# A gated mix of a state-space convolution and a dense layer: later signal stages, more store buffers, accumulators seeded by ScalarE, and a new list schedule

## The chip, the cores and the metric

The kernel runs on one core of a Trainium2 chip. The metric is device time in microseconds (us), the median of several runs. The core has a matrix engine (PE, with weight loads shown as PEld), a vector engine (DVE), a scalar engine (ACT), GpSimd (POOL) and SyncE (SP). SP does no arithmetic here; it issues most of the transfers, and POOL issues the rest. Each engine works through its own instructions in the order in which the program lists them.

## The reference

Input x is 2048 x 512 (sequence by channels). Three things are made of it and mixed:

```python
g = sigmoid((x * gate_w).sum(-1, keepdims=True))
# a: a long convolution over the sequence, one kernel K per channel (N = 128 states)
dt = exp(log_dt); P = exp((dt * A)[:, :, None] * l)       # complex, l = 0 .. 2047
K = einsum("dn,dnl,dn->dl", C, P, dt * B).real
a = irfft(rfft(pad(x)) * rfft(pad(K)))[:2048] + x * Dskip
# b: a dense layer of 512 -> 1792 -> 512
b = gelu(x @ w1 + b1) @ w2 + b2
out = g * a + (1 - g) * b
```

All numbers are 32-bit floats. b1 and b2 are the dense layer's two biases.

## The kernel before, in words

The program has two parts. The **front** (function `front`) runs the whole dense layer, builds the convolution's taps K, and puts both the signal and the taps through the first stage of a two-stage Fourier transform. The second part (`conv`) does the second stage, multiplies the spectra, transforms back, and adds the result to the output. `conv` is not touched by the change.

The dense layer keeps float32 accuracy by splitting every operand into a high part and a low rest (`split`: ACT or DVE casts the high part, DVE subtracts it for the rest). Each product then takes three matmuls: high x high, low x high, high x low. The sequence is cut into 8 blocks of 256 rows, and the 14 column tiles of the hidden layer into two halves of 7, so there are 16 passes (`NB`); in passes 0 to 7 the first half of w1 and w2 is resident, in 8 to 15 the second. A pass has four steps (`j` = 0 to 3) of 2, 2, 2 and 1 column tiles:

- `hidden` (matmuls in lines 899 to 901, 256 columns): 12 per column tile, into one of three PSUM banks `ph`. Then ACT applies gelu with bias b1 (line 916) and casts the high part `hh` (line 919), and DVE subtracts for `hl` (line 929).
- `output` (lines 947 to 949, 512 columns): three per column tile and row half, accumulated in two PSUM banks `acc`, one for each half of the block's 256 rows. After step 3, ACT scales the sum by (1 - g) into `io` (line 968) and it is stored. In passes 0 to 7 the accumulation starts with a matmul of a row of ones with b2 (line 942), the bias split in two parts as well (`bias`).

The taps take 16 chunks (`taps`): DVE and ACT build powers and rotations in `xc` and `y` (ACT's sines at lines 604 to 606, DVE's products up to line 667), and PE contracts them over the states (`contract`, line 681, 128 small matmuls into the bank `pk`). After every second chunk a **first stage** follows (`first_stage`, line 403): eight matmuls into four banks, one `ph`, the `pk` and two `pu`, each then copied out by ACT. The signal has eight first stages of its own (`signal`): two loads of rows of x into `ux` (line 417), the same eight matmuls, four copies by ACT into store buffers `st` (line 421), and stores to a scratch tensor `tu_d` (line 424). The buffers come from a ring of `N_ST`. Before `conv` begins, `early` reads 27 pieces of `tu_d` back into tiles called `attic`, `loft` and `den` (line 446). While the front runs, parts of these tiles serve for other things; so `attic` in a row of a profile is a store buffer, a load buffer or a `ux`, by the line that it stands with.

What sets the order is a list schedule made when the program is built. Every piece of work is a `Task` with an engine, an estimated duration, a due time and its dependencies. `Plan.run` walks the engines in time: of the tasks that are ready it takes the one with the earliest due time, adds its estimated duration, and the order found in this way is the order in which instructions are issued. Due times are linear in the step's number, bent by `warp`, with offsets: `U_0` and `U_GAP` set the signal's stages, `K_0` and `T_KG` the chunks of the taps, `T_0` and `T_MLP` the dense steps, `D_...` single kinds of task. These times are the plan's own and not the chip's.

Of the kernel before, what the change touches and what calls it, by code (L numbers as in the profile page):

```python
# [17 lines left out]
P = 128  # L18
L = 2048
D = 512  # L20
# [13 lines left out]
T_0 = 22.7  # L34
T_MLP = 411.78
K_0 = 24.88
T_KG = 373.15
U_0 = -15.83
U_GAP = 12.75
LAG = 12.23  # L40
TABLE = 9.03
D_KA = -63.09
D_KP = 0.01
D_S1 = 19.39
D_EV = -65.14
D_H = -60.13
D_LO = -10.68
PS = (2, 3, 1, 2)
N_ACC, N_H, N_PK, N_PU = PS
D_SP = 2.63  # L50
MEM = (6, 2, 3)
N_LD, N_HL, N_ST = MEM
D_XS = -33.08
D_G = 1.83
N_WARM = 13
T_EARLY, T_LOFT, T_DEN = 376.87, 422.84, 432.0
Y_K, Y_U = 41.11, 36.03
W_MLP = (-0.0634, -0.0326, 0.0273)
W_KG = (-0.0624, -0.0351, -0.0316)
W_U = (-0.058, -0.1265, 0.0001)  # L60
D_MAG = 0.58
D_ROT = 1.16
D_CON = 0.62
D_PHA = 0.72
D_PRE = 0.04
D_XL = -26.72
D_COE = 0.25
D_OUT = -5.37
N_LATE = 2
N_REST = 3  # L70
N_KEEP = 4

# [131 lines left out]
class Plan:  # L204
# [5 lines left out]
    def add(self, part, hold, fn, due, reads=(), writes=(), table=None, done=None, after=(), rows=1.0):  # L210
# [9 lines left out]
        t.rows = rows  # L220
# [10 lines left out]
    def run(self):  # L231
        clock = Clock()
        free = dict.fromkeys(("PE", "ACT", "DVE", "POOL", "SP", "GP"), 0.0)
# [4 lines left out]
        table, order, dma = None, [], 0.0  # L238
        for _ in self.tasks:
# [13 lines left out]
            hold = clock.run(at, t.hold, t.rows) if p == "PE" else t.hold  # L253
# [21 lines left out]
def gated_mix(  # L275
# [41 lines left out]
    def front(pool, psum, keep, attic, loft, den):  # L317
# [10 lines left out]
        def act(n, fn, due, reads=(), writes=(), table=None, ops=1):  # L328

            return pl.add("ACT", 0.1 * ops + n / 1200.0, fn, due, reads, writes, table)  # L330

        def mm(hold, fn, due, reads=(), writes=(), rows=1.0):

            return pl.add("PE", hold, fn, due, reads, writes, rows=rows)

        def move(kb, fn, due, reads=(), writes=(), queue="SP", after=()):

            hold = 0.45 if queue == "SP" else 1.0
            return pl.add(queue, hold, fn, due, reads, writes, done=kb / 360.0, after=after)
# [20 lines left out]
        st, ld = rooms[1 : 1 + N_ST], rooms[1 + N_ST : 1 + N_ST + N_LD]  # L360
        gwb = rooms[1 + N_ST + N_LD]
# [16 lines left out]
        b2r = pool.tile([P, D], F32R, name="b2r")  # L378
        ones = pool.tile([P, P], F32R, name="ones")
# [12 lines left out]
        def first_stage(xs, due, evac, ahead=2):  # L392
# [12 lines left out]
            mm(1.2, products, due + D_S1, [*(key for _, key in xs), "c1"], [key for _, key in banks], 0.5)  # L405
# [5 lines left out]
        def signal():  # L411
            for s in range(8):
# [6 lines left out]
                def evac(r, pp, key, s=s, t=t):  # L419
                    k = take("st", N_ST)  # L420
                    act(512, lambda: nc.scalar.copy(st[k], pp), t + D_EV, [key], [("st", k)])  # L421
# [9 lines left out]
        def early():  # L431

            us = places(attic, loft, den)
            keys = [("ux", 0)] + [("st", k) for k in range(N_ST)]
# [17 lines left out]
        def make_dt():  # L452
# [25 lines left out]
            act(4, lambda: nc.scalar.activation(r, r, AF.Exp, scale=0.25), -200, [], ["dt"], table="exp")  # L478
# [26 lines left out]
        def prepare(u, t, eb_k):  # L505
# [25 lines left out]
            act(7 * UW, scaled, act_due, ["pr"], ["xt"], ops=7)  # L531
# [6 lines left out]
            act(11 * UW, exps, act_due, ["pr"], [("ea", u % 2), kx], "exp", ops=11)  # L538
# [17 lines left out]
            act(18 * UW, sines, act_due, [], ["xt", "xv"], "sin", ops=3)  # L556
# [45 lines left out]
        def waves(t):  # L602
# [4 lines left out]

            act(99 * CW, sines, t + D_KA, ["ph"], ["tt"], "sin", ops=3)

        def begin(c, k, t):  # L610

            cs = slice(c * CW, (c + 1) * CW)
            act(
                8 * CW, lambda: nc.scalar.copy(xc[k][:, :, 0:4], x4[:, :, :, cs]), t + D_KA,  # L614
                ["x4"], [("xc", k)],
            )
# [54 lines left out]
        def contract(u, c, k, t):  # L671
# [18 lines left out]
            for g0 in (0, 4):  # L690
                mm(1.89, lambda g0=g0: products(g0), t + D_KP, ["y0", "y1", ("xc", k)], [("pk", q)])
# [8 lines left out]
            act(512, lambda: nc.scalar.copy(xs, pks[q].rearrange("p s g -> p (s g)")), t + D_S1, [("pk", q)], [key])  # L700
# [4 lines left out]
            def evac(r, pp, key):  # L705
                act(
                    512,
# [68 lines left out]
        def split(h, lo, src, hk, lk, key, due, on_vector=False):  # L776
            if on_vector:
                vec(512, lambda: nc.vector.tensor_copy(h, src), due, [key], [hk], fast=2)
            else:
                act(512, lambda: nc.scalar.copy(h, src), due, [key], [hk])  # L780
# [51 lines left out]
        def gates(b0, b1_, t):  # L832
# [3 lines left out]
                16, lambda: nc.scalar.activation(gate[:, 0, ts], gs[:, ts], AF.Sigmoid), t,  # L836
# [11 lines left out]
        def bias():  # L848

            k, q = take("ld", N_LD), take("ld", N_LD)  # L850
            one, b2f, keys = ld[k][:, 0:P], ld[q], [("ld", k), ("ld", q)]

            def fill():
                nc.gpsimd.memset(b2f, 0.0)
                nc.gpsimd.memset(one, 0.0)
                nc.gpsimd.memset(one[0:1], 1.0)
                nc.gpsimd.memset(one[32:33], 1.0)

            def rows():
                nc.sync.dma_start(b2f[0:1], b2)  # L860
                nc.sync.dma_start(b2f[32:33], b2)

            def go():
                nc.scalar.copy(ones, one)
                nc.scalar.copy(b2r, b2f)

            def low():
                nc.vector.tensor_sub(b2r[32:33], b2f[32:33], b2r[32:33].bitcast(F32))

# [468 lines left out]
```

## Time and profile before

| | |
|---|---|
| runs (us) | 539.93, 541.77, 539.12; median 539.93 |
| span of the profiled execution | 539.9 us, within 0.03 us of the median, so the two are used as one |
| instructions | 12181 |
| moved | 104.73 MB, mean 194 GB/s |
| first hidden matmul | 6.35 us |
| last hidden matmul, start | 424.25 us |
| first matmul of `conv` | 424.46 us |
| last matmul of the program, start | 528.15 us |

How the rows are read: a row of the page's groups has line, engine, operation, output <- inputs, shapes, count, then busy time, the mean of one in ns, and the idle time just before them with what ended it. A row of the timeline has its start, its duration and the instruction; `x4` means that four such are merged. Matmuls are pipelined, so a matmul's duration (0.28 or 0.39 us) is longer than its share of PE's time; the distance from one start to the next is that share. A row of waits has the waiting engine and line, what it waited for, the total, how often, and the longest. The granted clock is 1.00 when PE runs at full speed.

### The profile page before, as it was taken

The page shows a single profiled execution, that of the slowest core. Times are in us where ns is not written, and L with a number is a line of the kernel's source. Part 1 is how long each engine was busy: PE and PEld are TensorE (multiplying, and loading weights), DVE is VectorE, ACT ScalarE, POOL GpSimd, SP SyncE. Part 2 cuts the span into 40 slices and gives each one's busy share as a digit, 9 for nine tenths or more (in the row PEclk, how much of TensorE's full clock was granted, in tenths as well). Part 3 has the DMA queues.
Part 4 walks back from the last instruction along what each step waited for, and adds up shares of the span by engine and source line. Part 5 has one row for each costly group of instructions (what it writes and reads, how often), then busy time and mean ns, then how long its engine had stood idle before and what let it go on. Part 6 is the DMA issues. An engine that isn't in the chain of part 4 may idle for free.

```text
span 539.9 us, 12181 instructions
## 1 busy us (share of the span) xinstructions
PE 511.7 (95%) x4818; PEld 385.6 (71%) x4818; DVE 426.8 (79%) x806; ACT 353.5 (65%) x614; POOL 40.9 (8%) x79
## 2 busy tenths in 40 slices
PE   7878899999999999989999999999999999999981
PEld 7546789898899889777988989889888522223620
DVE  5898799999999959869999899999511388887132
ACT  4989846699875599976577987387253555555030
POOL 2000000000000000000102010101010001011040
PEclk9879999999999999999999999999999999999996
DMA  7989564162584442583887037514778758998888
GB/s 245 357 288 313 181 235 139 59 197 82 130 232 179 158 127 72 178 280 74 212 196 205 19 88 162 126 60 104 231 188 198 210 207 289 392 386 290 319 163 189
DMA packets 80837, 104.73 MB, mean 194 GB/s; under 512 B 39222, under 2 KB 43450, under 8 KB 80268
## 3 DMA queue, kind: packets, MB, share of 16 engines
q1 hardware_dynamic: 73756, 79.80, 46.7%
q0 software_dynamic: 6688, 21.79, 16.5%
q10 hardware_dynamic: 336, 2.36, 1.2%
q8 instruction: 38, 0.62, 0.4%
q14 instruction: 19, 0.16, 0.1%
HBM read 58.31 MB, written 45.62 MB: 192 GB/s over the span
## 4 chain that ended last, share of the span: by engine, by line
PE 76%; DMA 9%; ACT 8%; DVE 3%; issue 1%; SPq 1%; ACTq 0%; DVEq 0%
PE pk L681 10%; PE ph L899 8%; PE acc L947 8%; PE ph L901 8%; PE ph L900 8%; PE acc L949 7%; PE acc L948 7%; PE p2u L1108 5%; PE p2k L1108 5%; PE pa L1147 3%; PE pb L1236 3%; DMA tu_d<-attic 3%; DMA attic<-in_xs_dram 2%; PE ph L403 2%; ACT L916 1%
## 5 line engine op out<-in xcount | busy, mean ns | idle before, releaser
L899 PE MATMUL ph<-xh,wh 128*128 128x256 f32 x448 | 128.9, 288 | 3.4 <-ACT attic L421 2.2
L901 PE MATMUL ph<-xh,wl 128*128 128x256 f32 x448 | 127.6, 285 | 0.8 <-DVE wl L782 0.7
L900 PE MATMUL ph<-xlo,wh 128*128 128x256 f32 x448 | 127.2, 284 | 0.0
L899 PEld LDWEIGHTS ph<-xh,wh 128*128 128x128 f32 x448 | 85.8, 192 | 14.1 <-issue 5.6
L947 PE MATMUL acc<-wh,hh 128*128 128x512 f32 x210 | 85.1, 405 | 3.2 <-ACT hh L919 3.2
L900 PEld LDWEIGHTS ph<-xlo,wh 128*128 128x128 f32 x448 | 85.9, 192 | 2.0
L901 PEld LDWEIGHTS ph<-xh,wl 128*128 128x128 f32 x448 | 85.8, 191 | 1.6 <-DVE wl L782 1.6
L949 PE MATMUL acc<-wh,hl 128*128 128x512 f32 x210 | 83.2, 396 | 0.4 <-DVE hl L929 0.4
L948 PE MATMUL acc<-wl,hh 128*128 128x512 f32 x210 | 83.1, 396 | 0.0
L916 ACT ACTIVATE ph<-ph,b1t 128x256 f32<-128x256 f32 x112 | 50.4, 450 | 42.8 <-PE ph L901 40.8
L929 DVE TENSOR_TENSOR hl<-ph,hh 128x512 fp32r<-128x512 f32 (+1 forms) x62 | 38.5, 621 | 32.4 <-ACT hh L919 32.3
L681 PE MATMUL pk<-y,den 128*32 128x64 f32 x2048 | 61.4, 290 | 0.0
L681 PEld LDWEIGHTS pk<-y,den 128*32 128x32 f32 x2048 | 57.2, 136 | 3.7 <-issue 1.4
L947 PEld LDWEIGHTS acc<-wh,hh 128*128 128x128 f32 x210 | 39.7, 189 | 18.2 <-issue 6.8
L949 PEld LDWEIGHTS acc<-wh,hl 128*128 128x128 f32 x210 | 39.8, 190 | 11.0 <-DVE hl L929 2.1
L643 DVE TENSOR_TENSOR y<-y,ea 128x64 f32<-128x64 f32 (+4 forms) x80 | 45.5, 569 | 0.2
L948 PEld LDWEIGHTS acc<-wl,hh 128*128 128x128 f32 x210 | 39.8, 189 | 6.7
L919 ACT CAST hh<-ph 128x512 fp32r<-128x512 f32 (+1 forms) x62 | 33.0, 533 | 10.3 <-PE acc L948 6.9
L488 DVE TENSOR_TENSOR loft<-den,zz 128x256 f32<-128x256 f32 (+2 forms) x48 | 37.4, 779 | 2.7 <-ACT den L614 2.3
L489 DVE TENSOR_TENSOR loft<-den,zz 128x256 f32<-128x256 f32 (+2 forms) x48 | 37.3, 777 | 0.0
L656 DVE TENSOR_TENSOR y<-y,loft 128x2048 f32<-128x2048 f32 x16 | 36.6, 2288 | 0.0
L1116 ACT COPY k<-p2k 128x512 f32<-128x512 f32 x32 | 18.8, 586 | 25.0 <-issue 13.1
(178 smaller groups left out, 876.3 us busy)
## 6 DMA issues: line engine op xcount, KB each, us to landing
tu_d<-attic SPq DMA_DIRECT2D x64, 128.0 KB, 3.4
tk_d<-sk SPq DMA_DIRECT2D x32, 256.0 KB, 4.9
tk<-tk_d SPq DMA_DIRECT2D x32, 256.0 KB, 4.4
t_d<-sa SPq DMA_DIRECT2D x32, 256.0 KB, 4.8
t<-t_d POOLq DMA_DIRECT2D x9, 512.0 KB, 7.1
attic<-in_xt_dram SPq DMA_DIRECT2D x16, 256.0 KB, 3.8
xh_d<-xh SPq DMA_DIRECT2D x8, 512.0 KB, 3.4
xl_d<-xlo SPq DMA_DIRECT2D x8, 512.0 KB, 4.6
```

The costliest lines, as they stand in the source:

```text
L488: vec(2 * m, lambda: vv.tensor_mul(t, a, br), due, [ka, *kb], [kt])
L643: nc.vector.tensor_mul(both(n, 64 - 3 * n, n), both(0, 64 - n, n), an)
L681: nc.tensor.matmul(pks[q][32 * j : 32 * j + 32, :, gg], x[:, r, :, ch], y[:, r, :, ch], start=(r == 0), stop=(r == 1), skip_group_check=True,)
L899: nc.tensor.matmul(p, h, xh[xk][:, d], start=(d == 0), stop=False)
L900: nc.tensor.matmul(p, h, xlo[xk][:, d], start=False, stop=False)
L901: nc.tensor.matmul(p, lo, xh[xk][:, d], start=False, stop=(d == 3))
L916: nc.scalar.activation(phs[q][:, n], phs[q][:, n], AF.Gelu_apprx_tanh, bias=b1t[:, f : f + 1])
L929: nc.vector.tensor_sub(lo, phs[q][:, 0:nf], hi.bitcast(F32))
L947: nc.tensor.matmul(a, h, wh[1][w], start=start, stop=False)
L948: nc.tensor.matmul(a, h, wl[1][w], start=False, stop=False)
L949: nc.tensor.matmul(a, l, wh[1][w], start=False, stop=(j == 3))
L1108: nc.tensor.matmul(out[64 * i : 64 * i + 64], w, x, start=True, stop=True)
```

## The change

It has five parts.

- **The second bias.** The function `bias` and the matmul of ones with b2 are gone. b2 is loaded once, broadcast to all 128 partitions (`b2a`), and ACT copies it into an accumulator before the accumulation starts (`seed`): twice at the start, and right after the scaling of each block's sum in passes 0 to 6. The first output matmul then adds to what is there. The warm-up matmuls at the start now write the two accumulators rather than `pk`, twelve instead of thirteen.
- **The signal's first stage begins later**: `U_0` from -15.83 to 18.93.
- **Five store buffers** for three (`N_ST`), the two added ones are tiles of their own (`st`). The two halves of an evicted bank are stored by one transfer of 256 KB instead of two of 128 KB.
- **The gates** are computed in four batches instead of three, and the blocks at whose steps their dot products stand are listed (`DOTS_AT`).
- **The list schedule** of the front is made anew: almost all constants, the tasks' estimated durations, and a plan that knows two more things, a cost when PE changes between tiled and whole matmuls (`SWITCH`) and a limit of eight transfers under way per queue (`N_LANES`).

```diff
-U_0 = -15.83
-U_GAP = 12.75
+U_0 = 18.93
+U_GAP = 10.84
...
-MEM = (6, 2, 3)
+MEM = (6, 2, 5)
 N_LD, N_HL, N_ST = MEM
...
+DOTS_AT = (2, 6, 7, 8, 12, 18, 21, 23)
-N_WARM = 13
+N_WARM = 12
...
+N_LANES = 8
+SWITCH = 0.1
...
             if p in ("SP", "GP"):
                 dma = max(dma, at + 1.2) + t.done
-                end = dma + 0.9
+                end = dma + 1.2
+                landed[p].append(end)
+                if len(landed[p]) >= N_LANES:
+                    free[p] = max(free[p], landed[p][-N_LANES])
...
-        st, ld = rooms[1 : 1 + N_ST], rooms[1 + N_ST : 1 + N_ST + N_LD]
+        st, ld = rooms[1:4] + tiles(N_ST - 3, [P, D], "st"), rooms[4 : 4 + N_LD]
...
-                    for m in range(2):
-                        move(
-                            128, lambda m=m: nc.sync.dma_start(rows[:, 8 * s + 4 * m + r], st[k][64 * m : 64 * m + 64]),
-                            t, [("st", k)], [("u_d", 8 * s + 4 * m + r)],
-                        )
+                    at = rows[:, 8 * s + r : 8 * s + r + 5 : 4].rearrange("k m d -> m k d")
+                    move(
+                        256, lambda: nc.sync.dma_start(at, st[k]), t,
+                        [("st", k)], [("u_d", 8 * s + 4 * m + r) for m in range(2)],
+                    )
...
-        def bias():
...
+        def seed(q, due):
+
+            act(0.52, lambda: nc.scalar.copy(acc[q], b2a), due, ["b2a"], [("acc", q)])
...
-                start = j == 0
-                if start and b < NSB:
-                    nc.tensor.matmul(a, ones, b2r, start=True, stop=False)
-                    start = False
+                seeded = b < NSB
+                start = j == 0 and not seeded
...
                         t + D_EV, [("acc", q), ("gate", b % NSB)], [("io", r)],
                     )
+                    if b + 1 < NSB:
+                        seed(q, t + D_EV)
...
+            move(256, lambda: nc.sync.dma_start(b2a, b2.to_broadcast([P, D])), D_B2, [], ["b2a"])
...
-            pl.add("PE", 0.213 * N_WARM, warm, -200, ["dm"], [("pk", 0)])
+            pl.add("PE", 0.213 * N_WARM, warm, -200, ["dm"], [("acc", q) for q in range(N_ACC)])
+            for q in range(N_ACC):
+                seed(q, D_B2)
...
-            when = {1 + round(D_G * b): b for b in range(NSB)}
-            batches = {0: (0, 1), 2: (1, 3), 7: (3, 8)}
+            when = dict(zip(DOTS_AT, range(NSB)))
+            batches = {0: (0, 1), 2: (1, 3), 4: (3, 5), 7: (5, 8)}
```

The change's constants show little of what the new order is, so three places of it stand here. In these rows a number behind a name is a buffer's, and differs between the two programs for the same tile.

First place, ACT at the start of the program: the casts of x and of the weights (`xh`, `wh`), and the first gelu. Before:

```order
L780 CAST xh_106<-attic 128x512 x2
L780 CAST wh_110<-sk 128x512
L864 CAST ones<-attic 128x128
L865 CAST b2r<-attic 128x512
L780 CAST wh_117<-sk 128x512
L780 CAST wh_112<-sk 128x512
L780 CAST wh_118<-sk 128x512
L780 CAST wh_119<-sk 128x512
L780 CAST wh_114<-y 128x512
L916 ACT_TABLE_LOAD
L916 ACTIVATE ph_87<-ph_87,b1t 128x256 x2
L919 CAST hh_138<-ph_87 128x512
```

Now:

```order
L792 CAST xh_108<-attic 128x512 x2
L792 CAST wh_112<-sk 128x512
L862 COPY acc_85<-b2a 128x512
L862 COPY acc_86<-b2a 128x512
L792 CAST wh_119<-sk 128x512
L792 CAST wh_114<-sk 128x512
L905 ACT_TABLE_LOAD
L905 ACTIVATE ph_87<-ph_87,b1t 128x256 x2
L908 CAST hh_140<-ph_87 128x512
L792 CAST wh_120<-sk 128x512
L792 CAST wh_121<-sk 128x512
```

The two seeds stand where the bias was cast, and the first gelu has moved ahead of three weight casts.

Second place, ACT after the first block's gelus: the tables of the first taps (`loft<-pr`, `ea`, `den`). Before:

```order
L529 ACTIVATE loft<-pr 128x128 x7
L536 ACT_TABLE_LOAD
L536 ACTIVATE ea_98<-pr 128x128 x6
L536 ACTIVATE den<-pr 128x128 x5
L421 COPY attic<-ph_89 128x512
L421 COPY attic<-pk_90 128x512
L421 COPY attic<-pu_91 128x512
L552 ACTIVATE loft<-loft 128x768
L553 ACT_TABLE_LOAD
L553 ACTIVATE loft<-loft,half_pi 128x768
L554 ACTIVATE loft<-loft 128x768
L421 COPY attic<-pu_92 128x512
```

Now, up to the second block's first gelu:

```order
L548 ACT_TABLE_LOAD
L548 ACTIVATE ea_98<-pr 128x128 x6
L548 ACTIVATE den<-pr 128x128 x5
L848 ACT_TABLE_LOAD
L848 ACTIVATE gate<-gs 128x2
L564 ACTIVATE loft<-loft 128x768
L565 ACT_TABLE_LOAD
L565 ACTIVATE loft<-loft,half_pi 128x768
L566 ACTIVATE loft<-loft 128x768
L905 ACT_TABLE_LOAD
L905 ACTIVATE ph_88<-ph_88,b1t 128x256 x2
L908 CAST hh_140<-ph_88 128x512
```

The evictions of the signal's first stage (line 421, now 433) are gone from this place, and the first gate stands in it. Ahead of these rows stand, since the first block's last weight cast, the seven scalings, four casts of x for the second and third block, and the first block's last gelu.

Third place, SP, which issues the transfers, after the first weights. Before:

```order
L1002 DMA attic<-in_gw_dram 128x512
L1011 DMA dm<-in_dskip_dram 4x128
L417 DMA attic<-in_xl_dram 128x512
L417 DMA ux_103<-in_xl_dram 128x512
L773 DMA attic<-in_xt_dram 128x512 x2
L773 DMA attic<-in_xs_dram 128x512 x4
L417 DMA attic<-in_xl_dram 128x512
L417 DMA ux_103<-in_xl_dram 128x512
L773 DMA attic<-in_xs_dram 128x512
L424 DMA tu_d<-attic 64x512 x6
```

Now:

```order
L988 DMA attic<-in_gw_dram 128x512
L1000 DMA dm<-in_dskip_dram 4x128
L785 DMA attic<-in_xt_dram 128x512 x4
L429 DMA attic<-in_xl_dram 128x512
L429 DMA ux_105<-in_xl_dram 128x512
L785 DMA attic<-in_xs_dram 128x512 x2
L828 DMA xh_d<-xh_109 128x1024
L785 DMA attic<-in_xs_dram 128x512
L828 DMA xl_d<-xlo_111 128x1024
```

The x of the second and third block (`in_xt`) is now loaded ahead of the signal's rows (`in_xl`), and the stores of the signal's first stage (line 424, now 436) have left this stretch of the queue.

More of the change, by code (lines that the diff above doesn't have):

```diff
@@ L232, in run @@
         clock = Clock()
-        free = dict.fromkeys(("PE", "ACT", "DVE", "POOL", "SP", "GP"), 0.0)
+        free = dict.fromkeys(("PE", "ACT", "DVE", "POOL", "SP", "GP"), 0.75)
         ready = {p: [] for p in free}
@@ L237, in run @@
                 ready[t.part].append(t)
-        table, order, dma = None, [], 0.0
+        table, tiled, order, dma = None, False, [], 0.0
+        landed = {"SP": [], "GP": []}
         for _ in self.tasks:
@@ L252, in run @@
             ready[p].remove(t)
-            hold = clock.run(at, t.hold, t.rows) if p == "PE" else t.hold
+            hold = t.hold
+            if p == "PE":
+                turn = SWITCH if t.tiled != tiled else 0.0
+                tiled = t.tiled
+                hold = clock.run(at, turn + hold, t.rows)
             if t.table and t.table != table:
@@ L377, in front @@
         dm = pool.tile([P, P], F32, name="dm")
-        b2r = pool.tile([P, D], F32R, name="b2r")
-        ones = pool.tile([P, P], F32R, name="ones")
+        b2a = pool.tile([P, D], F32, name="b2a")
         dts = tiles(4, [P, 4], "dts")
@@ L477, in make_dt @@
             vec(300, before, -200, [], ["dt"])
-            act(4, lambda: nc.scalar.activation(r, r, AF.Exp, scale=0.25), -200, [], ["dt"], table="exp")
+            act(0.1, lambda: nc.scalar.activation(r, r, AF.Exp, scale=0.25), -200, [], ["dt"], table="exp")
             vec(400, behind, -200, [], ["dt"])
@@ L706, in evac @@
                 act(
[L707 removed]
+                    0.48,
                     lambda: nc.scalar.copy(
@@ L846, in gates @@
             )
-        def bias():
[L850 to L868, printed above, removed]
-            pl.add("POOL", 0.5, fill, -99, [], keys)
-            pl.add("SP", 0.9, rows, -98.5, [], keys, done=0.1)
-            act(640, go, 0, keys, ["b2"], ops=2)
-            vec(512, low, 0, keys, ["b2"])
+        def seed(q, due):
+            act(0.52, lambda: nc.scalar.copy(acc[q], b2a), due, ["b2a"], [("acc", q)])
         def cols(i):
```

125 lines of the change are left out of this document (62 added, 63 removed).

## The prediction

> **What bounds the kernel now.** I read the page's busy shares first, then the stretches, then PE's waits early and late. The page, under 1:
>
> ```profile
> PE 511.7 (95%) x4818; PEld 385.6 (71%) x4818; DVE 426.8 (79%) x806; ACT 353.5 (65%) x614; POOL 40.9 (8%) x79
> ```
>
> PE leads, but a mean hides where time is lost. The stretches (start:end, length, then busy time and count of each engine, granted clock, DMA share, GB/s):
>
> ```profile
> 6.35:15.40 9.05, 7.17 (x48) 6.13 (x49) 6.63 (x12) 4.28 (x8) 0.57 (x1) 1.00 0.94 307
> 15.40:17.80 2.40, 0.44 (x4) 0.12 (x2) 2.00 (x5) 2.32 (x5) 0.00 (x0) 1.00 1.04 399
> 17.80:22.70 4.90, 4.90 (x13) 3.60 (x14) 4.49 (x9) 4.84 (x14) 0.68 (x2) 0.65 1.04 375
> ...
> 28.40:36.40 8.00, 4.11 (x16) 0.69 (x16) 7.87 (x22) 7.69 (x10) 0.00 (x0) 0.77 0.94 289
> 36.40:41.00 4.60, 4.53 (x30) 4.39 (x36) 4.14 (x7) 2.33 (x4) 0.00 (x0) 0.65 0.95 342
> ...
> 80.00:120.00 40.00, 40.00 (x475) 35.53 (x474) 40.00 (x77) 29.85 (x51) 0.25 (x2) 1.00 0.43 140
> ...
> 200.00:240.00 40.00, 40.00 (x408) 34.76 (x401) 32.57 (x70) 36.42 (x71) 1.31 (x4) 1.00 0.54 175
> ```
>
> From 80 us on PE is filled at full clock (two of the rows shown). Before that it idles, the clock is granted at 0.65 to 0.77 in three stretches, and DMA is near its limit. So the front, up to its last matmul, is PE-bound behind a bad first 66 us. How bad needs PE's own pace:
>
> ```profile
> 60.84 0.39 PE L948 MATMUL acc<-wl,hh 128*128 128x512 f32 x1
> 61.07 0.39 PE L949 MATMUL acc<-wh,hl 128*128 128x512 f32 x1
> ...
> 95.03 0.64 PE L403 MATMUL ph<-s,c1t 32*64 32x512 f32 x2
> ...
> 96.07 0.50 PE L947 MATMUL acc<-wh,hh 128*128 128x512 f32 x1
> ...
> 253.37 0.28 PE L900 MATMUL ph<-xlo,wh 128*128 128x256 f32 x1
> ...
> 253.49 0.28 PE L901 MATMUL ph<-xh,wl 128*128 128x256 f32 x1
> ```
>
> Start to start, a 512-column matmul takes 0.23 to 0.235 us, a 256-column one 0.12 (0.1175 over longer runs), a whole first stage 1.04. What PE did up to 66 us (groups in that window, with their counts and idle time):
>
> ```profile
> L899 PE MATMUL ph<-xh,wh 128*128 128x256 f32 x56 | 17.1, 306 | 3.4 <-ACT attic L421 2.2 <-DVE wh L778 1.1
> ...
> L947 PE MATMUL acc<-wh,hh 128*128 128x512 f32 x20 | 8.5, 427 | 2.0 <-ACT hh L919 2.0
> L949 PE MATMUL acc<-wh,hl 128*128 128x512 f32 x19 | 8.2, 430 | 0.0
> ...
> L403 PE MATMUL pu<-attic,c1t 32*64 32x512 f32 x12 | 6.2, 691 | 2.4 <-ACT attic L421 2.4
> ...
> L403 PE MATMUL ph<-attic,c1t 32*64 32x512 f32 x6 | 3.2, 608 | 1.4 <-DMA attic<-in_xl_dram 1.4
> L942 PE MATMUL acc<-b2r,ones 128*128 128x512 f32 x4 | 1.9, 480 | 1.8 <-ACT io L968 1.8
> ```
>
> 168 hidden matmuls (3 x 56) x 0.1175 = 19.7; 58 output ones (20 + 19 + 19) x 0.235 = 13.6; 4 bias ones 0.9; three first stages 3.1. That is 37.4 us of work in the 59.7 us from the first hidden matmul at 6.35: **22.3 us lost**. The rows name 10.9 us of waits; the low clock cost 4.9 x 0.35 + 8.0 x 0.23 + 4.6 x 0.35 = 5.2. After 66 us PE waits by the list for just this:
>
> ```profile
> PE acc L947 <- ACT hh L919: 1.2, 1, 1.2
> PE acc L949 <- DVE hl L929: 0.4, 1, 0.4
> ```
>
> The contractions, on the page:
>
> ```profile
> L681 PE MATMUL pk<-y,den 128*32 128x64 f32 x2048 | 61.4, 290 | 0.0
> ```
>
> That is 3.84 us for each of the 16 (128 matmuls). The same sum for 66 to 424.4 us, by the loops' counts, gives 1176 x 0.1175 + 572 x 0.235 + 61.4 + 13 x 1.04 + 12 x 0.235 = 350.3 of 358.4: 8.1 us of small overheads. The second part (424.5 on) is the same code before and after.
>
> **The change part by part.** *The bias matmuls go.* 16 at 0.235 us: **-3.8**, all on PE while it is full. In their place ACT makes 16 copies 128x512. A PSUM to SBUF copy of that size is in this row, with a table load:
>
> ```profile
> 39.15 0.59 ACT L421 COPY attic<-pu 128x512 f32<-128x512 f32 x1 [2.25 <-DMA tu_d<-attic]
> 39.76 1.28 ACT L916 ACT_TABLE_LOAD   x1
> 41.05 0.45 ACT L916 ACTIVATE ph<-ph,b1t 128x256 f32<-128x256 f32 x1
> ...
> 41.80 1.14 ACT L780 CAST xh<-attic 128x512 fp32r<-128x512 f32 x2
> ```
>
> No copy of 512 elements into PSUM stands in this trace. Its bounds are the 0.45 of the half-sized gelu, which does write PSUM, and the 0.64 of a scaled read out of it (1.28 for two, below); I take the 0.59 of the copy the other way, 9.4 us in all. The new order has 54 table loads on ACT for 47: 7 x 1.28 = 9.0. Against that go two casts of the old bias. ACT stands at 65%, so I put these 18 us at nothing on the path, the cover being PE's other hidden and output work; without cover they are a rival, below. One rule speaks against these loads: the Trainium skill, "ScalarE: Activation LUTs", section "What ACT_TABLE_LOAD costs", adds a drain of about 1.38 us to each load. Here the load ends at 41.04 and the next activation starts at 41.05, so no drain shows; by the Trainium skill's figure the seven would be 18.6 us, an estimate, and the sum would still not move while they are covered.
>
> *The signal's first stage moves behind the first block.* Its first three stages stood behind 12, 15 and 18 us of PE's work, now behind 29, 39 and 51. Stalls it caused before 66 us: 2.4 + 2.2 + 1.4 = 6.0 us named, two of the three low-clock stretches (1.8 + 1.6), and much of the unnamed rest. Its evictions waited for a store buffer:
>
> ```profile
> ACT attic L421 <- DMA tu_d<-attic: 12.0, 6, 6.1
> ```
>
> With five buffers for a stage's four evictions, and stages further apart, a stage no longer waits for its own stores. The 2.0 us wait for hh at 15.4 goes too, since the gelu is now ahead of the casts of late weights (order rows, first place), and with it probably the low clock behind it (1.7).
>
> What is left of the 22.3? (a) Start-up: 48 hidden matmuls are 5.6 us of work in the 9.05 of the first stretch, so 3.4 lost to weights arriving and being split. The broadcast of b2 puts 256 KB ahead of all weights but one, 0.66 us at the 399 GB/s of the next stretch: 4.1. (b) ACT's queue between the first block's last hidden matmul and the second block's first gelu (second place). Its prices:
>
> ```profile
> 21.67 1.51 ACT L529 ACTIVATE loft<-pr 128x128 f32<-128x128 f32 x7
> ...
> 24.49 1.31 ACT L536 ACTIVATE ea<-pr 128x128 f32<-128x128 f32 x6
> ...
> 28.21 0.87 ACT L552 ACTIVATE loft<-loft 128x768 f32<-128x768 f32 x1
> ...
> 30.39 0.94 ACT L553 ACTIVATE loft<-loft,half_pi 128x768 f32<-128x768 f32 x1
> ...
> 46.26 0.93 ACT L916 ACTIVATE ph<-ph,b1t 128x256 f32<-128x256 f32 x2
> ...
> 59.53 1.28 ACT L968 ACTIVATE io<-acc,gate 128x512 f32<-128x512 f32 x2
> ```
>
> A last weight cast 0.6, seven scalings 1.5, four x casts 2.3, a half gelu and cast 0.8, exp load and 11 exps (1.31 for six) 3.7, sigmoid load and a small gate 1.5, abs, sine load and two sines 4.0, gelu load, gelu and cast 2.8, and DVE's subtraction 0.6: 17.8 us. PE has 30 output and 72 hidden matmuls there, 7.0 + 8.5 = 15.5, and then needs that bank: a wait of 2.3. Behind it ACT has a gelu and cast, two scalings and two seeds, 1.5 + 1.3 + 1.1 = 3.9, before block two's first output matmul, PE 12 hidden ones and a first stage, 2.4: 1.5 more. Sum of (a) and (b) 7.9, so the early loss falls by **14.4**. Bounds: nothing of (b), 4 us better; or ACT stays late for the next two blocks as well, 10 us worse.
>
> A rule on the clock bears on (b). The rows: 2.40 us with hardly any matmul were followed by 4.90 at a clock of 0.65. The Trainium skill, "TensorE: Matmul & The Clock Gate", section "What's actually happening", has the clock halve after a whole idle window of about 3.4 us. By it the 2.3 us gap of (b) costs no clock; by the row it would cost some 1.7 us more, which lies inside my range.
>
> *Stores of 256 KB for two of 128.* 32 instead of 64, freeing SP issue slots; after 66 us PE waits for no transfer (the two rows above), so nothing. Were SP late, the next block's x would be, which stands in the same queue.
>
> *The list made anew.* PE's earlier front asks DVE to deliver earlier. The rotation's last product and the contraction behind it:
>
> ```profile
> 253.57 1.22 DVE L667 TENSOR_TENSOR y<-y,loft 128x1024 f32<-128x1024 f32 x1
> 254.78 0.45 PE L681 MATMUL pk<-y,den 128*32 128x64 f32 x8
> ...
> 386.75 1.31 PEld L681 LDWEIGHTS pk<-y,den 128*32 128x32 f32 x48 [0.36 <-issue]
> ```
>
> y is ready just when PE takes it (254.79 and 254.78). In the new order 120 hidden and 42 output matmuls and a first stage follow the last contraction: 14.1 + 9.9 + 1.0 = 25 us, for 34 before. With the sum so far the front would end at 424.4 - 18.2 = 406.2 and the last contraction start at 406.2 - 25 - 3.8 = 377.4, 9.4 us ahead of now. DVE's idle time would have to give that: 7.4 us of it lie in 200 to 240 alone. Bounds 0 and 9.4; I take **+3.5**, nearer to free, since that stretch alone holds most of it.
>
> *The seam.* From the last first stage to the second part:
>
> ```profile
> 411.26 1.30 SPq L1086 DMA_DIRECT2D cc<-in_c_dram  x1
> 414.59 1.75 SPq L1089 DMA_DIRECT2D tk<-tk_d  x4
> ...
> 424.46 1.08 PE L1108 MATMUL p2k<-tk,cc 128*64 128x512 f32 x4
> ```
>
> The taps are read from 414.6 on, some 10 us ahead of use. The new order has 22.4 us of PE work behind the last first stage for about 25, and three more 256 KB loads between its stores: I take **+1** (0 to 4).
>
> Sum against the profiled execution's span of 539.9 us (median of the runs 539.93, nothing to convert): 539.9 - 3.8 - 14.4 + 3.5 + 1.0 = **526.2 us**.
>
> **The rivals.** *DVE sets the taps' pace* (20%): it delivers the last y when it does now, PE's front ends at 386.8 + 3.8 + 25 = 415.6, and the total is 539.9 - 8.8 + 1 = 532, whatever PE has won before. For it: DVE is at 40.00 of 40 from 80 to 120 us. Against: its idle time at 200 to 240.
> *The stalls only move* (14%): ACT is late for block two and three, (b) grows from 3.8 to 14 us; 526.2 + 10 = 536. For it: the ACT queue above, and ACT's 4.84 of 4.90 at 17.8. Against: from 80 to 120 us ACT is busy for 29.85 of 40.
> *The seam opens* (8%): the eight stores and the loads behind them take the 13 us from 411 to 424 again and start no earlier against PE's shorter cover; PE waits 5, total 526.2 - 1 + 5 = 530.
> *ACT's seeds hold PE; slower* (6%): at the end of a block both accumulators need scaling and seeding in ACT's in-order queue before the next block's first output matmul. Two of each are 1.3 + 1.1 = 2.4 us; a sigmoid load and gate and a gelu load ahead of them make 5.2. At seven block ends that is 17 to 36 us if PE has no hidden block ready to cover it; from 2.6 us per block the 18 us gained are gone. At 3.5 us each the total is 526.2 + 24.5 - 3.5 (DVE then has time) = 547. For it: the bias matmul already waited 1.8 us for the scaling once. Against: once in 14 times, and each accumulator's seed is issued right behind its scaling.
> *Forecast* (52%).
>
> **How the numbers follow.** The forecast's own terms span 518 (nothing of DVE's, the seam's and (b)) to 531; with DVE's rival and most of the moved stalls the range is 520 to 534.5, leaving out the slower case, part of the moved stalls, and the case that nothing at all is lost. Within 0.5% means 537.2 to 542.6, about what a measurement of this kernel can tell from no change. Faster: 52 + 20 + 8 + 8 of the 14 = 88%; same: the other 6; slower 6.
>
> **What would show it.** No bias row; PE's first 66 us losing 8 us, not 22; no wait of the store eviction on its own stores; clock 1.00 from about 45 us on; last hidden matmul at about 410, last contraction near 381. Wrong if "acc <- ACT" waits appear at block ends (seeds), if contractions wait for y (DVE), or the first p2k waits for tk.

## The result, and the profile after

| | us, median (runs) | ratio to the kernel before, 95% interval |
|---|---|---|
| before, beside it | 540.38 (539.12 to 541.77, 4 runs) | 1 |
| the change | 581.64 (578.12 to 583.89, 4 runs) | 1.0739 [1.0701, 1.0777] |

The kernel became 7.4% slower. The forecast was 526.2 us, its range ended at 534.5, and it gave a slower kernel a chance of 6%.

The page after, parts 1 and 4 (busy time; then the chain that ended last, by line):

```profile
PE 514.4 (88%) x4800; PEld 388.6 (67%) x4800; DVE 427.2 (73%) x806; ACT 370.4 (64%) x636; POOL 39.7 (7%) x75
...
PE pk L693 6%; DMA tu_d<-attic 6%; PE acc L931 5%; PE p2u L1097 5%; PE p2k L1097 5%; PE acc L932 5%; PE acc L933 5%; PE ph L888 4%; PE ph L890 4%; PE ph L889 4%; DMA attic<-in_xs_dram 3%; DMA pr<-in_prm_dram 3%; PE pa L1136 3%; PE pb L1225 3%; DMA attic<-in_w_dram 2%
```

PE's 95% has become 88%, and a store, `tu_d<-attic`, whose data is first read back at 329 us stands in the chain that ended last with 6%. The stretches of the kernel after (columns as in the prediction):

```profile
17.80:22.70 4.90, 4.80 (x34) 4.32 (x33) 4.09 (x9) 1.97 (x5) 0.67 (x2) 1.00 1.02 304
28.40:36.40 8.00, 8.00 (x59) 7.58 (x59) 7.96 (x26) 7.91 (x18) 0.00 (x0) 1.00 1.02 369
...
56.00:58.00 2.00, 2.00 (x11) 1.64 (x10) 1.93 (x4) 2.00 (x3) 0.00 (x0) 1.00 0.13 51
...
78.00:83.00 5.00, 5.00 (x18) 3.54 (x12) 3.85 (x7) 1.17 (x2) 0.00 (x0) 0.52 0.13 51
80.00:120.00 40.00, 32.56 (x382) 27.46 (x380) 17.79 (x34) 23.41 (x33) 0.25 (x2) 0.88 0.37 131
```

Up to 40 us it went as forecast: in 28.4 to 36.4, where PE had worked 4.11 us at a clock of 0.77, it is full at 1.00. Then come stretches such as 56 to 58 us in which DMA moves 51 GB/s at a share of 0.13, about two sixteenths, for whole microseconds. In 80 to 120 us, full before, PE works 32.56 us and DVE 17.79 of 40. SP's queue tells what these stretches are:

```profile
48.01 5.17 SPq L436 DMA_DIRECT2D tu_d<-attic  x3
53.28 4.85 SPq L436 DMA_DIRECT2D tu_d<-st  x1
58.22 4.93 SPq L828 DMA_DIRECT2D xh_d<-xh  x1
...
63.78 3.15 SPq L785 DMA_DIRECT2D attic<-in_xs_dram  x2
```

They are the joined stores of the signal's first stage (line 436). 256 KB at 51 GB/s take 5.1 us, the four of a stage 20.6. SP is held while it issues them, and what stands behind them is late: here x. The rows of the store itself, before (line 424) and after, give the time for which one issue held SP (min/median/max in ns): before,

```profile
L424 SPq DMA_DIRECT2D tu_d<-attic x64: 445/588/5339, 28.3 to 269.1; - x64
```

and after,

```profile
L436 SPq DMA_DIRECT2D tu_d<-attic x20: 487/2734/6412, 48.0 to 305.1; - x20
```

The rate has an explanation in the Trainium skill, "DMA: Bandwidth & Descriptors", section "Why a DMA increments its semaphore by 16 and not by 1": a transfer gets the largest number of engines, up to 16, that divides the outermost dimension of both its sides. The joined store's scratch side is 2 x 64 x 512, so by that rule it gets 2 of 16; the share of 0.13 agrees.

This reaches PE in two ways. The first, through what stands behind the stores, is plainest late in the front. First SP, then DVE, then PE, all of the kernel after:

```profile
262.21 9.02 SPq L436 DMA_DIRECT2D tu_d<-attic  x3
271.32 3.33 SPq L522 DMA_DIRECT2D pr<-in_prm_dram  x1
```

```profile
289.19 0.69 DVE L530 TENSOR_TENSOR pr<-pr,dtb 128x512 f32<-128x512 f32 x1 [11.56 <-DMA pr<-in_prm_dram]
```

```profile
294.15 1.11 PE L415 MATMUL ph<-attic,c1t 32*64 32x512 f32 x1 [11.90 <-DVE hl L915]
```

Three stores hold SP for 9.02 us, the load of the taps' parameters `pr` stands behind them, DVE waits 11.56 us for it with all its later work, the rest `hl` for the dense layer among it, and PE waits 11.9 us for that. SP is through with this load at 274.65, yet its data are used only at 289.19. So holding SP is the smaller part of the delay; the load lands late too. By an estimate from 5.1 us a store, the four stores issued from 261.6 on last until 282. PE's list of waits never names a transfer of the front; it names DVE and ACT:

```profile
PE ph L415 <- DVE hl L915: 11.9, 1, 11.9
PE ph L415 <- ACT s L712: 11.9, 2, 9.6
PE ph L888 <- DVE hl L915: 7.4, 2, 5.5
PE acc L931 <- ACT hh L908: 6.8, 1, 6.8
PE pk L693 <- ACT attic L433: 4.2, 1, 4.2
```

One step further back DVE's own list has the transfers:

```profile
DVE attic L838 <- DMA attic<-in_xs_dram: 15.7, 4, 9.9
...
DVE pr L530 <- DMA pr<-in_prm_dram: 12.0, 2, 11.6
```

The second way goes through the store buffers, and the chain of the kernel after shows it early in the front (a transfer's piece runs from its issue to its landing):

```profile
49.31 17.03 DMA tu_d<-attic
...
73.49 18.43 DMA tu_d<-attic
...
115.82 9.38 DMA attic<-in_xs_dram
...
156.57 9.89 DMA attic<-in_xs_dram
...
243.94 12.82 DMA attic<-in_w_dram
...
271.32 17.78 DMA pr<-in_prm_dram
```

The first two pieces are stores, and behind each ACT evicts the next stage's bank into the buffer that the store had held. Even five buffers are not enough: in the third stage the last three evictions start at 81.75, 86.88 and 92.00 us, one for each 5.1 us in which a store lands. ACT then does its gelus late, and PE waits for what follows from them: 5.5 us (`hl`) behind the second stage's evictions and 6.8 us (`hh`) behind the third's. The other four pieces are loads. Of PE's five waits of over 4 us, the two behind stores make 12.3 us and the three behind loads 25.7 (9.6, 4.2 and 11.9).

### The profile page after: what moved, and what is told of

It is laid out like the page before. It is cut to its first block, busy times and chain, and to the rows that moved or that the text cites. A ratio compares the mean times of both kernels' runs of the same rounds, so it can differ in the third digit from the quotient of the medians.

```text
span 581.6 us, 12113 instructions
## 1 busy us (share of the span) xinstructions
PE 514.4 (88%) x4800; PEld 388.6 (67%) x4800; DVE 427.2 (73%) x806; ACT 370.4 (64%) x636; POOL 39.7 (7%) x75
## 3 DMA queue, kind: packets, MB, share of 16 engines
q0 software_dynamic: 6688, 21.79, 15.4%
## 4 chain that ended last, share of the span: by engine, by line
PE 51%; DMA 21%; ACT 16%; DVE 6%; issue 2%; SPq 1%; ACTq 0%; DVEq 0%
PE pk L693 6%; DMA tu_d<-attic 6%; PE acc L931 5%; PE p2u L1097 5%; PE p2k L1097 5%; PE acc L932 5%; PE acc L933 5%; PE ph L888 4%; PE ph L890 4%; PE ph L889 4%; DMA attic<-in_xs_dram 3%; DMA pr<-in_prm_dram 3%; PE pa L1136 3%; PE pb L1225 3%; DMA attic<-in_w_dram 2%
## 5 line engine op out<-in xcount | busy, mean ns | idle before, releaser
L931 PE MATMUL acc<-wh,hh 128*128 128x512 f32 x210 | 88.3, 420 | 9.9 <-ACT hh L908 6.8
L932 PE MATMUL acc<-wl,hh 128*128 128x512 f32 x210 | 84.4, 402 | 0.0
L931 PEld LDWEIGHTS acc<-wh,hh 128*128 128x128 f32 x210 | 41.0, 195 | 34.3 <-issue 13.2
L932 PEld LDWEIGHTS acc<-wl,hh 128*128 128x128 f32 x210 | 41.2, 196 | 6.7
L1105 ACT COPY k<-p2k 128x512 f32<-128x512 f32 x32 | 18.7, 586 | 25.5 <-issue 13.1
```

The source lines that it names most:

```text
L931: nc.tensor.matmul(a, h, wh[1][w], start=start, stop=False, skip_group_check=seeded)
L932: nc.tensor.matmul(a, h, wl[1][w], start=False, stop=False, skip_group_check=seeded)
```

## The experiments

The theory to test, **A**: the joined store is slow by its shape (the outermost dimension of 2), and this alone turns a gain into a loss; the rest of the forecast holds. The rivals: it is the size or the number of the transfers; or the joining as such; or the new order is bad in itself. A kernel called "with halves" is the change with two stores of 128 KB. In the code cuts of this part lines are shortened, and others are left out.

### Two stores for each bank again

```diff
-at = rows[:, 8 * s + r : 8 * s + r + 5 : 4].rearrange("k m d -> m k d")
-nc.sync.dma_start(at, st[k])
+for m in range(2):
+    nc.sync.dma_start(rows[:, 8 * s + 4 * m + r], st[k][64 * m : 64 * m + 64])
```

> The changed kernel, but each evicted bank is stored as before by two transfers of 128 KB (64 partitions each) at the place of the one of 256 KB; list order, five buffers, seeds as in the change. Theory A (the joined transfer has a slowest dimension of 2 on the scratch side, so it runs on two of the 16 DMA engines, 51 GB/s, and everything behind it in SP's queue is late): the stalls of 65 to 300 us go, DMA share never sits at 0.13, and the time falls from 582 to 522 to 535, near the forecast of 526. Theory B (the new list itself is bad: ACT and DVE late after the seeds and table loads): it stays over 560. Theory C (both): 540 to 560.

Measured: **525.25 us** (524.45 to 526.02, 4 runs), ratio 0.9715 [0.9683, 0.9748]. One edit that moves no other instruction is worth 56 us, and what is left lies near the forecast. The stretches of this kernel:

```profile
28.40:36.40 8.00, 8.00 (x59) 7.54 (x58) 7.97 (x26) 7.91 (x19) 0.00 (x0) 1.00 1.02 378
...
80.00:120.00 40.00, 40.00 (x486) 35.00 (x485) 39.91 (x74) 35.46 (x66) 0.25 (x2) 1.00 0.42 134
200.00:240.00 40.00, 39.00 (x380) 32.88 (x379) 37.10 (x73) 38.59 (x75) 2.24 (x5) 1.00 0.67 184
```

PE is full at full clock in 28.4 to 36.4 us already, and in 80 to 120 again, where the change had lost it. The new order is thus not bad in itself.

### The same 128 KB, cut the other way

Two stores of 128 KB per bank, but each takes half of the columns of both parts, so each has a scratch side of 2 x 64 x 256.

```diff
+for h in range(2):
+    hs = slice(256 * h, 256 * h + 256)
+    nc.sync.dma_start(at[:, :, hs], st[k][:, hs])
```

> The changed kernel with two transfers of 128 KB per bank, but cut by columns, so that each still has a slowest dimension of 2. Theory A (the slowest dimension sets the number of DMA engines, size does not matter): as slow as the change, 575 to 600, DMA share again near 0.13 while a store is alone. If it is the size of 256 KB or the single issue that costs: as fast as with two halves of 64 partitions, under 540.

Measured: **591.51 us** (590.15 to 592.88), ratio 1.0936 [1.0881, 1.0991]. Its stretch beside the stores:

```profile
54.00:56.00 2.00, 2.00 (x10) 1.67 (x9) 1.93 (x5) 1.99 (x3) 0.00 (x0) 1.00 0.14 49
```

Size and count are those of the fast kernel, and the rate is that of the slow one. Size and count fall as causes. Why it takes 10 us more than the change stays open.

### The joined store in the kernel before

The kernel before, with the joined store and nothing else of the change.

> The kernel before with only the joined store, at the place of the second of its two halves; order else unchanged. Theory A: eight stages of four stores, 32 x 5.1 us on two DMA engines = 164 us, and with three buffers ACT's evictions and SP's queue wait for them: 40 to 80 us slower, 580 to 620. Theory B: no change, 536 to 544.

Measured: **609.29 us** (609.25 to 609.32), ratio 1.1264 [1.1216, 1.1312]. The harm doesn't need the new order; with three buffers and an early signal it is larger.

### Outermost dimension of 4, and of 16

One store of 256 KB in both, into scratch rows that are numbered in another way; what `conv` reads is thus permuted, and the output of these two kernels is not the reference's.

```diff
+h = slice(32 * (s % 2), 32 * (s % 2) + 32)
+at = rows[h, 16 * (s // 2) + r : 16 * (s // 2) + r + 13 : 4].rearrange("k m d -> m k d")  # 4 x 32 x 512
...
+at = rows[8 * s : 8 * s + 8, r : r + 61 : 4].rearrange("k m d -> m k d")  # 16 x 8 x 512
```

> One transfer of 256 KB for each evicted bank, as in the change, but its scratch side is 4x32x512 and not 2x64x512 (four groups of 32 partitions go to four scratch rows in steps of four, two stages filling the rows between them). The scratch rows then hold the signal's first stage in another arrangement, so what the second part reads is permuted; sizes, counts and the order of the work are the change's. Theory A (the number of DMA engines a store gets is the extent of the outermost dimension of its scratch side): a share of about 0.25 (4 of 16 engines) and about 102 GB/s while such a store runs alone, 2.6 us for each, 10 us for a stage; SP is held half as long as in the change, and the time lies between 526 and 550 us. Theory B (it is the joining of two strided parts in one transfer that is slow, whatever their number): as in the change, about 582.

> As the kernel before this one in the list, with a scratch side of 16x8x512 (sixteen groups of eight partitions), still one transfer of 256 KB for each bank; permuted scratch rows again. Theory A: all 16 DMA engines, no stores visible as a floor of the share at 0.13, and the time of two stores of 128 KB, 525 us (523 to 527). Theory B (joined transfers are slow): about 582. A third view, that one 256 KB transfer is by itself better than two of 128 KB because it halves SP's issue slots: 1 us or more below 525.

Measured: **534.58 us** with 4 (534.23 to 534.92), ratio 0.9869 [0.9825, 0.9913]; **522.89 us** with 16 (521.39 to 525.72, 4 runs), ratio 0.9658 [0.9615, 0.9701]. While stores of the first of them run alone:

```profile
53.00:55.00 2.00, 2.00 (x23) 1.77 (x29) 1.90 (x6) 1.95 (x5) 0.00 (x0) 1.00 0.26 100
```

and the same part of the second, where they run beside loads:

```profile
50.00:52.00 2.00, 2.00 (x19) 2.00 (x17) 1.53 (x5) 1.90 (x6) 0.00 (x0) 1.00 1.05 401
```

So a joined transfer isn't slow. With 2, 4 and 16 the time is 581.6, 534.6 and 522.9 us, and the lone share 0.13 and 0.26: theory A, also in its proportion. Whether one store of 16 x 8 x 512 beats two of 128 KB is not settled: the intervals of their ratios overlap.

### The joined store, issued by POOL

```diff
-256, lambda: nc.sync.dma_start(at, st[k]), t,
+256, lambda: nc.gpsimd.dma_start(at, st[k]), t,
```

> The change as it is, its joined stores of 256 KB with a scratch side of 2x64x512 too, but issued by POOL and not by SP: SP's queue then carries loads and the other stores only. Theory A1 (the harm goes through SP's in-order queue: the loads of x and of the taps' parameters stand behind the slow stores, while nobody reads the stores themselves before some 330 us): 523 to 535 us, whether the stores' own share stays at 0.13 (then ScalarE's evictions still wait for buffers now and then) or not. Theory A2 (the stores' own lateness does it, by the buffers that they hold): 550 us or more, as long as their share stays at 0.13. If POOL's queue spreads the same pattern over more engines than SP's, A1 and A2 are not told apart, and the time is about 525.

Measured: **534.28 us** (531.83 to 538.20, 4 runs), ratio 0.9892 [0.9825, 0.9958]. The stores still landed late, here from issue to landing in the last column (us),

```profile
tu_d<-attic POOLq DMA_DIRECT2D x20, 256.0 KB, 12.7
...
tu_d<-st POOLq DMA_DIRECT2D x12, 256.0 KB, 13.4
```

against 3.6 and 3.4 in the kernel with halves, and yet 47 of the 56 us are back. (Of the change's own stores the trace has no such medians; two in its chain took 17.0 and 18.4 us.) One longer wait is left on PE:

```profile
PE ph L888 <- DVE hl L915: 8.0, 2, 5.8
```

It is the buffers' way once more: the wait of 5.8 us ends at 71.25 us, and before it the evictions of the second stage start at 61.82, 64.39 and 67.03 us, each waiting for a store. The waits behind loads are gone. That fits A1 for the greater part of the harm, as PE's waits in the kernel after do. But this run does not separate A1 from A2 by itself. Buffers come free 2.6 us apart here, and 5.1 apart in the change, and ACT waits 7.1 us for its own stores instead of 18.5. The share of 0.13 isn't seen either; while SP issues nothing, from 66 to 68 us, it is 0.52. So moving the stores to POOL eased the buffers as well, and the rate of a single store in POOL's queue wasn't measured.

### The second bias: no seeds, and matmuls instead

Both are the kernel with halves, with the order of the rest as it was. The first leaves out the second bias. The second also casts the bias in two parts at the start, where the first seed stood.

```diff
-act(0.52, lambda: nc.scalar.copy(acc[q], b2a), due, ["b2a"], [("acc", q)])
+act(0.52, lambda: None, due, ["b2a"], [("acc", q)])
...
+if start and b < NSB:  # in the second of the two kernels alone
+    nc.tensor.matmul(a, ones, b2r, start=True, stop=False)
```

> The change with two stores of 128 KB per bank, and without the 16 seeds: the second bias is left out of the result, the accumulation starts with its first product; b2 is still loaded, and every other instruction keeps its place. The forecast's price for the seeds is nothing on the path: 525.2 us, 524.2 at the lowest. Rival (seeds hold PE at block ends): 3 us or more faster.

> The change with two stores of 128 KB per bank, and the second bias added by 16 matmuls of ones with b2 as in the kernel before, in place of the 16 copies by ScalarE; every other instruction keeps its place. The forecast's term for the bias: 16 x 0.235 = 3.8 us more, 529.0 us. Rival (that time of PE is not on the path, because DVE sets the pace of the taps): 525 to 526.

Measured side by side: **523.38 us** without seeds (521.19 to 525.12, 6 runs), ratio 0.9660 [0.9630, 0.9691]; **528.23 us** with matmuls (527.05 to 530.60, 6 runs), ratio 0.9759 [0.9731, 0.9788]. The last hidden matmul of three kernels is a finer measure, since the front alone is changed: with seeds, without, and with matmuls,

```profile
404.55 0.28 PE L893 MATMUL ph<-xh,wl 128*128 128x256 f32 x1
```

```profile
404.72 0.28 PE L893 MATMUL ph<-xh,wl 128*128 128x256 f32 x1
```

```profile
408.55 0.28 PE L895 MATMUL ph<-xh,wl 128*128 128x256 f32 x1
```

Seeds or none differ by 0.2 us, matmuls cost 3.8 to 4.0. The forecast had nothing for the one and 3.8 for the other. These are single executions, though, and two other kernels of much the same order, with seeds, have this matmul at 405.44 (b2 behind the second weight, below) and 405.68 us (16 x 8 x 512), so the traces show the price of the seeds to no better than about 1 us. The medians agree: matmuls cost 4.9 us more than no seeds, side by side, and 3.0 more than seeds in another session; seeds and none, also in two sessions, are 1.9 us apart.

### The signal early again, and three buffers

Both are the kernel with halves, with the list made anew.

```diff
-U_0 = 18.93
-U_GAP = 10.84
+U_0 = -15.83
+U_GAP = 12.75
...
-MEM = (6, 2, 5)
+MEM = (6, 2, 3)
```

> The change with two stores of 128 KB per bank, and the signal's due times put back to the first kernel's (start -15.83, spacing 12.75); five store buffers, seeds and all else stay, the list is made anew with it: the first three first stages then stand behind about 9, 14 and 18 us of PE's work, as before the change. Theory A (the later start is what ended the early loss): the stalls of the first 66 us come back, about 8 us, 533 us (529 to 537). Rival (five buffers and the earlier gelu ended it): 524 to 527.

> The change with two stores of 128 KB per bank, but three store buffers; the list is made anew with it, the signal's stages stand where the change has them. Theory A (the later start counts, the buffers little): 525 to 528, with waits of the store's eviction on its own stores again, in ScalarE's queue but not in PE's. Rival (the buffers count): 531 us or more, with PE waiting for banks that are not evicted.

Measured: **550.10 us** with the early signal (547.26 to 551.38, 4 runs), ratio 1.0157 [1.0119, 1.0194]; **530.90 us** with three buffers (529.88 to 532.59, 4 runs), ratio 0.9812 [0.9781, 0.9844]. The early signal's waits on PE, and its stretch from 40 to 60 us:

```profile
PE ph L415 <- DMA attic<-in_xl_dram: 4.9, 1, 4.9
PE ph L415 <- DMA ux<-in_xl_dram: 4.8, 1, 4.8
...
PE ph L891 <- ACT st L433: 3.1, 1, 3.1
```

```profile
40.00:60.00 20.00, 12.21 (x57) 9.00 (x58) 17.20 (x42) 17.52 (x26) 0.56 (x1) 0.74 0.93 292
```

With the signal early, PE waits for the signal's rows while DMA is at a share of 0.93, and the clock falls to 0.74: the stalls of before, and worse. By the counts of its matmuls up to 66 us (168 hidden, 48 output, three first stages, 34.1 us of work) it loses 25.5 us there, for 22.3 before and 7.3 with halves. So 18 of the 25 us lie in the stretch that theory A names, which the later start had rid of its stalls; but 8 us in all were expected, and 550 is outside A's range. That constants made for a late signal give a poor list for an early one is my explanation, and not tested. The three buffers cost 5.6 us, between the two theories. Neither the 528 of the one nor the 531 of the other is met. PE waits mostly for `hl`, and once more for an eviction, though not of the signal's banks but of the taps' (`sk`); with halves these waits are 0.3 and 1.9 us, and the last is not there:

```profile
PE ph L415 <- DVE hl L918: 3.4, 2, 2.6
PE ph L891 <- DVE hl L918: 2.3, 1, 2.3
PE ph L891 <- ACT sk L723: 2.2, 2, 1.8
```

ACT waits 1.0 us for the signal's own stores, as theory A had it.

Since the list was made anew, how much of the 5.6 us is the buffers' and how much the list's stays open.

### b2 later in the queue

In the kernel after the first hidden matmul starts at 7.95 us, for 6.35 before, and I put this to the broadcast of b2 ahead of the weights.

```diff
-D_B2 = -98.57
+D_B2 = -97.5   # behind the second weight; in another kernel -96, behind the fourth
```

> The change with two stores of 128 KB per bank, and the broadcast of b2 issued behind the second weight instead of the first; the two seeds move behind one more weight cast on ScalarE, nothing else moves. Theory (the broadcast shares the bandwidth with the first weights and so delays the first hidden matmul by 1.6 us): that matmul starts 0.5 us or more before the 8.17 us that it had, and the time falls by as much, 524.7. Rival (what is won at the start is lost in the next wait): 525.3.

> As the kernel before it in the list, with b2 behind the fourth weight and the two seeds behind the first gelu; the list is made anew with it, which moves some later rows as well. Theory: the first hidden matmul at about 6.6 us, and the time 1.6 us lower, 523.6. Rival: 525.3, or anything within 2 us of it that the moved rows make.

Measured: **523.87 us** (522.04 to 524.92, 6 runs), ratio 0.9680 [0.9652, 0.9707]; **528.49 us** (528.05 to 531.90, 6 runs), ratio 0.9781 [0.9750, 0.9813]. The first hidden matmul starts at 6.79 and 7.35. But it starts at 6.53 in the kernel with 16 x 8 x 512, whose early order is the change's own:

```profile
6.53 0.38 PE L888 MATMUL ph<-xh,wh 128*128 128x256 f32 x1 [0.34 <-ACT wh L792]
```

So this start moves by up to 1.6 us between executions of one early order, and the theory isn't shown. In the first of the two the gain is gone by the last hidden matmul anyway (405.44, with halves 404.55), and its ratio's interval overlaps that of the kernel with halves. In the second the list moved too, and the time is 3.2 us longer than with halves.

## Why the prediction was wrong

**The step that failed** is "*Stores of 256 KB for two of 128.* 32 instead of 64, freeing SP issue slots; after 66 us PE waits for no transfer (the two rows above), so nothing." It measured +59.2 us by the spans (581.6 and 522.4) and +56.4 by the medians. Three things are wrong in it. It counted transfers and took the rate as given, while the edit changes the pattern: the diff's `rearrange("k m d -> m k d")` puts a dimension of 2 outermost, and the store then ran at 51 GB/s. Nor were issue slots freed: one issue held SP for 2.7 us in the median, for 0.59 before. And it argued from waits that the profile of before doesn't have, which says what the old transfers cost, not the new ones. The next sentence named the path ("Were SP late, the next block's x would be"), but with no price and no chance.

The other steps, by the kernel with halves (profiled span 522.4 us). The times from its first to its last instruction are compared here on both sides. In every run that has both figures the device time is 1.7 to 2.8 us longer than this span, so the forecast's "nothing to convert" was most likely a slip: the span of 539.9 agrees with the median of 539.93 presumably because a longer execution was profiled, and 526.2 as a span is some 528 as a device time.

| step | forecast | measured |
|---|---|---|
| bias matmuls go, seeds cost nothing | -3.8 | -3.8 to -4.0 |
| early loss of 22.3 us | -14.4 | -15.0 |
| DVE keeps the taps back | +3.5 | none seen |
| seam | +1.0 | +1.3 |
| sum on 539.9 | 526.2 | 522.4 |

That the measured column adds up to 522.4 exactly is luck, with single executions that differ by about 1 us. By medians side by side the gain is 16.1 us (541.36 and 525.25) and not 17.5; the forecast had 13.7.

- **Early loss.** Work up to 66 us, in the same groups as before:

```profile
L893 PE MATMUL ph<-xh,wl 128*128 128x256 f32 x84 | 25.1, 298 | 0.0
...
L934 PE MATMUL acc<-wh,hh 128*128 128x512 f32 x28 | 11.2, 399 | 0.0
```

252 x 0.1175 + 84 x 0.235 + 3.1 = 52.4 of the 59.7 us from 6.35 on: 7.3 are lost, where the forecast left 7.9 of 22.3. Up to 15.4 us, its (a), 37 hidden matmuls were done and 4.7 us lost (forecast 4.1); behind that, its (b), 2.6 (forecast 3.8). Of (b), the wait of 2.3 us for the second block's `hl` is there with 1.9, second row:

```profile
PE ph L891 <- ACT wh L795: 2.9, 1, 2.9
PE ph L891 <- DVE hl L918: 1.9, 1, 1.9
PE pb L1228 <- DVE loft L1242: 1.7, 2, 0.9
PE p2k L1100 <- DMA tk<-tk_d: 1.3, 1, 1.3
...
PE acc L934 <- ACT acc L865: 0.5, 1, 0.5
```

The clock stayed at 1.00 across PE's gap of about 2 us at 40 us, so the 1.7 us that the low clock after a gap might have cost did not come.

- **Seeds.** The last row is all that PE waited for them, 0.5 us, at the start. The 16 copies took 9.2 us on ACT (forecast 9.4). The rival that had the kernel slower by its seeds falls: the time did go up, but by another mechanism.
- **DVE.** The last contraction begins at 375.53 us in the kernel with halves, at 386.75 before; the forecast had 377.4 with DVE free and 380.9 with its term. No wait for `y` stands among PE's, so the 3.5 us were too many, and DVE did not set the taps' pace, as that rival had it.
- **Seam.** `p2k` waits 1.3 us for `tk` (fourth row), forecast 1, where "the first p2k waits for tk" had been named as a sign of error; it is one in the size of a few tenths.

Of the signs named, the joined store broke three. The last hidden matmul starts at 463.55 us and not at about 410, the clock is not 1.00 from 45 us on (0.52 from 78 to 83), and the store evictions do wait for their own stores; in ACT's waits of the kernel after stands, for 12.0 before,

```profile
ACT attic L433 <- DMA tu_d<-attic: 15.9, 4, 4.5
```

with 2.6 us more for `tu_d<-st`. With halves no such wait is left, and the last hidden matmul starts at 404.55 us, 59.0 earlier: the 59.2 us lie in the front.

## What to carry to other kernels

When an edit joins, splits or transposes a transfer, read the outermost dimension of both its access patterns before counting bytes: here 2, 4 and 16 gave 581.6, 534.6 and 522.9 us with the same bytes in the same order. A slow store on an in-order queue costs what is queued behind it, even if its own data is not wanted for hundreds of microseconds; the same store on another queue cost 9 us and not 56, with its buffers free twice as fast there. A slow store also keeps its buffer, and the engine that fills the buffers comes late. And where a list of waits names a compute engine, ask what that engine waited for: here the cause stood steps back, in DVE's and ACT's lists, never in PE's.

## What was not expected of the hardware

- A store with an outermost dimension of 2 ran at a DMA share of 0.13 and 51 GB/s, one of 4 at 0.26 and 100 GB/s.
- The first hidden matmul of one early order started anywhere from 6.53 to 8.17 us, and in the latter execution the clock of the first stretch was 0.62:

```profile
6.35:15.40 9.05, 7.23 (x37) 7.01 (x38) 4.47 (x8) 5.59 (x9) 0.71 (x1) 0.62 0.99 307
```

What sets this start wasn't found out.
